# Dummy matmuls in the opening of an attention and SwiGLU kernel: one in fp32 for every four in bf16

## The chip, the cores and the metric

The kernel runs on one core of one Trainium2 chip. The metric is the device time of one execution in microseconds (us). Several executions are timed; the median is quoted. A ratio is the mean time of one kernel's fast runs over that of the other's fast runs in the same rounds, so it is not quite the ratio of the medians quoted beside it. Brackets after a ratio hold its 95% interval. One early execution of the kernel before took 565.97 us; it is no fast run and enters no ratio, though the medians of 3 and 4 runs below count it.

## The reference

Causal attention over a sliding window of 64 keys, for 8 batches of 8 heads with 576 tokens and head size 64. Then a SwiGLU block with 512 model and 1536 hidden columns.

```python
scores = q @ k.transpose(0, 1, 3, 2) / sqrt(D)
mask = (rel >= 0) & (rel < 64)               # rel = query position - key position
attn = softmax(where(mask, scores, -1e9))
x = (attn @ v).transpose(0, 2, 1, 3).reshape(B * S, H * D)
g = x @ w_gate
out = (g * sigmoid(g) * (x @ w_val)) @ w_out
```

## The kernel before

The matmuls run in bf16. Inputs arrive in fp32, are cast on VectorE (DVE), ScalarE (ACT) or GpSimd (POOL), and queries and keys of the opening are transposed on TensorE (PE). While the first loads are still coming, PE is given dummy matmuls on zeros, so that its clock is released and stays released.

```python
wz = cst.tile([P, 512], BF16, name="wz")
...
def warm(n):
    w_ps = ps_f.tile([P, 512], FP32, name="w_ps", tag="g")
    for _ in range(n):
        nc.tensor.matmul(w_ps[:], wz[:, 0:P], wz[:])

def begin():
    dve.memset(wz[:], 0.0)
    make_identity(nc, identb[:])
    dve.memset(masks[0][:], 1.0)
    ...
# the opening (cut to the dummies and what stands beside them)
cast_k(0, "k_f", pool)
warm(11)
turn2(0, "k_f", (act, dve))      # transposes of the first keys
...
warm(3)
turn2(0, "q_f", (act, dve))
warm(3)
scores(0, True)
...
warm(7)
turn2(1, "k_f", act)
...
warm(4)
products(1)
...                              # then warm(1), warm(2), warm(2)
```

`keys_last` is a VectorE copy of keys that a transposing DMA has just been asked for:

```python
finish()
if n + 4 < NG // 2:
    turn1(n + 4, "k_f")          # DMA transposes
    keys_before(n + 4)
    keys_last(n + 4)             # copy on VectorE
project(t - 1, s)
```

The softmax here doesn't subtract the row's maximum and nothing guards it: scores larger than these inputs give would overflow.

## Time and profile before

| | before |
|---|---|
| median | 338.15 us (337.53 at best), 3 runs |
| span of the profiled run | 336.3 us |
| PE busy | 97% of the span |
| PE idle in the first 35 us | 5.65 us |
| PE idle from 36 us to its last matmul (333.2 us) | 0.76 us, one wait |

PE sets the time. Apart from 3.0 us after its last matmul, its idle time is almost all in the first 35 us, where it waits for casts and those for loads. The prediction shows the lines. The table of waits between 254 and 268 us names its parts (columns: who waited for whom, us in total, times, longest):

```profile
DVE kL L145 <- DMA kT<-k_fb: 3.4, 1, 3.4
PE g_ps L316 <- DVE sg L327: 0.8, 1, 0.8
```

VectorE stands in `keys_last` for 3.4 us until a transposing DMA lands; behind it in VectorE's order stands the gate multiplication (sg) that would free PE's next PSUM buffer.

### The profile page before, as it was taken

Reading aid. Unit: us, or ns where it says so; the run is one execution under the profiler, and the core shown is the slowest. Engines: PE = TensorE matmul, PEld = TensorE weight load, DVE = VectorE, ACT = ScalarE, POOL = GpSimd, SP = SyncE. Lnnn points to the kernel's source line nnn. Section 1 sums busy time; section 2 is a strip of 40 time slices with the busy share of each in tenths; the row PEclk is TensorE's granted clock in tenths of the full one; section 3 lists DMA queues with packets and bytes.
Section 4 is the critical chain, followed back from the end, with each engine's and each line's share of the span. In section 5 each row is a group of like instructions: output and inputs, shape, how many; then the busy total and the mean of one; then the engine's idle time right before and its main releaser. Section 6 shows DMA issues by size and latency. Waiting matters only on the chain.

```text
span 336.3 us, 7201 instructions
## 1 busy us (share of the span) xinstructions
PE 326.8 (97%) x2731; PEld 163.3 (49%) x2731; DVE 227.5 (68%) x491; ACT 152.0 (45%) x268; POOL 100.8 (30%) x148
## 2 busy tenths in 40 slices
PE   7898999999999999999999999999999999999996
PEld 3555665545544444444444444444444444444444
DVE  4667898995676767677868677767665866655520
ACT  3858876566525252534343434343433434232222
POOL 4543455661053333333333333223333110000000
DMA  8999999979968988899889698979998420211013
GB/s 207 266 308 283 309 274 320 317 168 230 206 137 166 181 165 172 165 188 167 178 174 168 152 180 175 164 141 214 146 188 137 101 64 32 65 31 31 33 47 109
DMA packets 150610, 56.83 MB, mean 169 GB/s; under 512 B 124720, under 2 KB 144560, under 8 KB 150576
## 3 DMA queue, kind: packets, MB, share of 16 engines
q1 hardware_dynamic: 150576, 56.38, 77.5%
q8 instruction: 21, 0.34, 0.5%
q14 instruction: 13, 0.11, 0.2%
HBM read 37.75 MB, written 9.44 MB: 140 GB/s over the span
## 4 chain that ended last, share of the span: by engine, by line
PE 85%; DMA 7%; ACT 2%; DVE 2%; SPq 1%; issue 1%; DVEq 0%; ACTq 0%
PE g_ps L316 26%; PE o_ps L334 26%; PE v_ps L316 25%; DMA q_f<-in_q_dram 3%; PE ao_ps L252 3%; PE s_ps L221 2%; DMA v_f<-in_v_dram 2%; PE tp L170 1%; DMA kT<-k_fb 1%; ACT E L234 1%; SPq L89 1%; DMA out_dram<-os__4900 1%; DVE sg L327 1%; PE xtp L276 1%; ACT ve L118 0%
## 5 line engine op out<-in xcount | busy, mean ns | idle before, releaser
L316 PE MATMUL g_ps<-xT,wg 128*128 128x512 bf16 (+1 forms) x460 | 112.4, 367 | 1.3 <-DVE sg L327 1.3
L316 PE MATMUL v_ps<-xT,wv 128*128 128x512 bf16 (+1 forms) x460 | 112.1, 366 | 0.5 <-POOL wv L120 0.3
L327 DVE SCALAR_TENSOR_TENSOR sg<-th,g_ps 128x512 f32<-128x512 f32 (+1 forms) x115 | 75.0, 652 | 52.1 <-ACT th L321 51.9
L321 ACT ACTIVATE th<-g_ps 128x512 f32<-128x512 f32 (+1 forms) x115 | 65.8, 573 | 77.6 <-PE g_ps L316 74.9
L334 PE MATMUL o_ps<-wo,hT 128*128 128x512 bf16 (+2 forms) x456 | 98.5, 368 | 0.0
L328 DVE TENSOR_TENSOR hT<-sg,v_ps 128x512 bf16<-128x512 f32 (+1 forms) x115 | 75.4, 655 | 11.9 <-PE xtp L276 0.5
L316 PEld LDWEIGHTS <-wv 128*128 128x128 bf16 x460 | 44.6, 98 | 49.6 <-ACT wv L118 0.7
L334 PEld LDWEIGHTS <-hT 128*128 128x128 bf16 x456 | 43.6, 98 | 49.5
L316 PEld LDWEIGHTS <-wg 128*128 128x128 bf16 x460 | 41.8, 98 | 43.4 <-issue 1.7
L234 ACT ACTIVATE E<-s_ps 128x512 bf16<-128x512 f32 x72 | 38.6, 596 | 8.1 <-PE s_ps L221 8.0
L120 POOL CAST q_fb<-q_f 128x1024 bf16<-128x1024 f32 x13 | 13.7, 1050 | 63.4 <-DMA q_f<-in_q_dram 37.9
L120 POOL CAST k_fb<-k_f 128x1024 bf16<-128x1024 f32 (+1 forms) x16 | 16.0, 1003 | 55.5 <-DMA k_f<-in_k_dram 44.2
L263 DVE TENSOR_TENSOR x_b<-ao_ps,r 128x256 bf16<-128x256 f32 x72 | 30.6, 425 | 2.5
L236 DVE TENSOR_TENSOR E<-E,mask 128x512 bf16<-128x512 bf16 x58 | 25.8, 472 | 9.0 <-ACT E L234 8.3
L120 POOL CAST ve<-v_f 64x512 bf16<-64x512 f32 x47 | 29.3, 623 | 2.9
L120 POOL CAST vo<-v_f 128x512 bf16<-128x512 f32 x30 | 19.0, 634 | 30.0 <-DMA v_f<-in_v_dram 29.8
L262 DVE RECIPROCAL r<-ao_ps 128x4 f32<-128x4 f32 x72 | 12.5, 174 | 4.6 <-PE ao_ps L252 4.6
L252 PEld LDWEIGHTS <-E 128*64 128x64 bf16 x576 | 11.0, 110 | 7.6 <-issue 5.8
L120 POOL CAST vL<-v_f 64x512 bf16<-64x512 f32 x15 | 9.3, 621 | 11.3 <-DMA v_f<-in_v_dram 10.5
L221 PEld LDWEIGHTS <-kT 64*128 64x128 bf16 x512 | 9.1, 95 | 5.7 <-issue 3.0
L252 PE MATMUL ao_ps<-vo,E 128*64 128x65 bf16 x256 | 11.9, 196 | 0.0
L252 PE MATMUL ao_ps<-ve,E 128*64 128x65 bf16 x256 | 11.9, 196 | 0.0
(100 smaller groups left out, 143.9 us busy)
## 6 DMA issues: line engine op xcount, KB each, us to landing
v_f<-in_v_dram SPq DMA_DIRECT2D x32, 256.0 KB, 4.5
k_f<-in_k_dram SPq DMA_DIRECT2D x20, 256.0 KB, 4.1
q_f<-in_q_dram SPq DMA_DIRECT2D x18, 256.0 KB, 5.1
q_f<-in_q_dram SPq DMA_DIRECT2D x7, 512.0 KB, 7.1
k_f<-in_k_dram SPq DMA_DIRECT2D x6, 512.0 KB, 7.4
w_f<-in_moe_w_gate_dram SPq DMA_DIRECT2D x6, 512.0 KB, 6.8
w_f<-in_moe_w_val_dram SPq DMA_DIRECT2D x6, 512.0 KB, 6.8
wo_f<-in_moe_w_out_dram SPq DMA_DIRECT2D x6, 512.0 KB, 7.2
```

The source lines that it names most:

```text
L120: eng.tensor_copy(y, x)
L221: nc.tensor.matmul(ps[a][:, p, b], keys, qT[g // 2 % QR][y, p, o:o + 64], tile_position=(64 * a, 0), start=not masked, stop=not masked or ...
L234: act.activation(e, x[:], AF.Exp, scale=0.125)
L236: dve.tensor_mul(e, e, mk[:].unsqueeze(1).to_broadcast([P, 4, 2, 64]))
L252: nc.tensor.matmul(o_ps[64 * b:64 * b + 64, i, :], Es[g % ER][:, y, b], z[:, y, :], tile_position=(0, 64 * b),)
L262: dve.reciprocal(r[:], o_ps[:, :, D])
L263: dve.tensor_mul(xb[g][:, 256 * h:256 * h + 256].rearrange("r (y d) -> r y d", y=4), o_ps[:, :, 0:D], r[:].unsqueeze(2).to_broadcast([P, 4 ...
L316: nc.tensor.matmul(ps[:, 0:n], w[:, c, P * m:P * m + P], xT[t][:, c, c0:c0 + n], start=(c == 0), stop=(c == 3),)
L321: act.activation(th[:, 0:n], g_ps[:, 0:n], AF.Tanh, scale=0.5)
L327: dve.scalar_tensor_tensor(sg[:, 0:n], th[:, 0:n], 1.0, g_ps[:, 0:n], ALU.add, ALU.mult)
L328: dve.tensor_mul(hT[t][:, m, c0:c0 + n], sg[:, 0:n], v_ps[:, 0:n])
L334: nc.tensor.matmul(o_ps[:, a:b], hT[t][:, c, P * s:P * s + P], wo[:, c, a:b], start=(c == 0), stop=(c == 11),)
```

## The change

Intent: an fp32 matmul of 512 columns keeps the array as long as four in bf16, with fewer instructions. PE's blocks of instructions then last longer while loads crowd the DMA engines.

```diff
     wz = cst.tile([P, 512], BF16, name="wz")
+    wz4 = cst.tile([P, 512], FP32, name="wz4")
...
     def warm(n):
         w_ps = ps_f.tile([P, 512], FP32, name="w_ps", tag="g")
-        for _ in range(n):
-            nc.tensor.matmul(w_ps[:], wz[:, 0:P], wz[:])
+
+        for z in [wz4] * (n // 4) + [wz] * (n % 4):
+            nc.tensor.matmul(w_ps[:], z[:, 0:P], z[:])
 
     def begin():
 
         dve.memset(wz[:], 0.0)
+        dve.memset(wz4[:], 0.0)
```

## The prediction

> **What bounds the kernel now.** I read the page first, then PE's instructions in order of time, then those of the other engines at the same moments. From the page (busy time by engine, the span in 40 slices, the DMA queues, the chain that ended last):
>
> ```profile
> PE 326.8 (97%) x2731; PEld 163.3 (49%) x2731; DVE 227.5 (68%) x491; ACT 152.0 (45%) x268; POOL 100.8 (30%) x148
> PE   7898999999999999999999999999999999999996
> DMA  8999999979968988899889698979998420211013
> q8 instruction: 21, 0.34, 0.5%
> PE 85%; DMA 7%; ACT 2%; DVE 2%; SPq 1%; issue 1%; DVEq 0%; ACTq 0%
> ```
>
> PE is the bound: it works from about 35 us to the end without a pause. Only the first four slices (8.4 us each) leave it idle time, and only there do the dummies run. So the change can act on the end only by moving the moment at which PE becomes saturated. PE in order of time, with the idle time before a group in brackets, says what holds it until then (columns: start, length, engine, line, what, count):
>
> ```profile
> 1.26 3.83 PE L347 MATMUL w_ps<-wz 128*128 128x512 bf16 x11 [1.26 <-DVE wz L351]
> 6.20 0.62 PE L170 MATMUL tp<-identb,k_fb 128*128 128x128 bf16 x8 [1.10 <-POOL k_fb L120]
> 9.43 1.68 PE L347 MATMUL w_ps<-wz 128*128 128x512 bf16 x7
> ...
> 12.74 0.62 PE L170 MATMUL tp<-identb,q_fb 128*128 128x128 bf16 x8 [0.95 <-DVE q_fb L120]
> ...
> 13.67 1.04 PE L347 MATMUL w_ps<-wz 128*128 128x512 bf16 x4
> ...
> 20.71 0.61 PE L316 MATMUL v_ps<-xT,wv 128*128 128x256 bf16 x4 [0.28 <-POOL wv L120]
> ...
> 23.81 1.02 PE L316 MATMUL g_ps<-xT,wg 128*128 128x512 bf16 x4 [0.51 <-DVE sg L327]
> ...
> 27.21 0.62 PE L170 MATMUL tp<-identb,q_fb 128*128 128x128 bf16 x8 [1.07 <-ACT q_fb L118]
> ```
>
> With two small ones not shown (0.16 before L208 at 16.25, 0.17 before L316 at 33.44) these pauses sum to 1.26+1.10+0.95+0.16+0.28+0.51+1.07+0.17 = 5.50 us. The table of seven windows of 5 us gives PE 29.34 us busy out of the first 35, so 5.66 idle: all but 0.16 us has a named data producer. I checked each producer's end against PE's start:
>
> ```profile
> 5.10 1.04 POOL L120 CAST k_fb<-k_f 128x1024 bf16<-128x1024 f32 x1 [0.91 <-DMA k_f<-in_k_dram]
> 19.61 1.04 POOL L120 CAST wv<-w_f 128x1024 bf16<-128x1024 f32 x1 [1.51 <-DMA w_f<-in_moe_w_val_dram]
> 26.54 0.62 ACT L118 CAST q_fb<-q_f 128x512 bf16<-128x512 f32 x1 [1.07 <-DMA q_f<-in_q_dram]
> ```
>
> 5.10+1.04 = 6.14 against 6.20; 19.61+1.04 = 20.65 against 20.71; 26.54+0.62 = 27.16 against 27.21. Each handover takes 0.05 to 0.06 us, and each cast waited for a load. The opening is bound by **loads**, and no pause is left that a late block of instructions could own.
>
> **What the Trainium skill says.** (1) "Runtime: NRT & Kernel Launch", section "Instruction fetch mechanics": instructions come in 16 KiB blocks of 256 through a DMA queue of the sequencer's own, the next block while the current one runs, mostly hidden. The trace agrees: 0.34 MB in 21 packets is 16 KiB each, PE's 2731+2731 = 5462 instructions are 21.3 such blocks, and no PE pause is unexplained. (2) "TensorE: Matmul & The Clock Gate", Part 1: the array runs at half clock until about 3.4 us of activity released it. The trace agrees: the first weight loads of the dummies start 0.43 us apart, and the last four lie within 0.80:
>
> ```profile
> 2.09 0.15 PEld L347 LDWEIGHTS <-wz 128*128 128x128 bf16 x1 [0.28 <-issue]
> 2.52 0.15 PEld L347 LDWEIGHTS <-wz 128*128 128x128 bf16 x1 [0.28 <-issue]
> 3.80 0.80 PEld L347 LDWEIGHTS <-wz 128*128 128x128 bf16 x4 [0.28 <-issue]
> ```
>
> The pitch of a 512-column matmul is thus 0.43 us cold and, from the L316 groups late in the chain (0.86 us for four), 0.216 warm; the clock is released near 4.1 us. (3) "FP8 and Floating Point Precision", section "TensorE Precision Notes": true FP32 takes four passes. The trace before has no fp32 matmul, so it cannot confirm it. (4) The clock-gate page, "Weight-path perf modes": the fast weight load is off for FP32. Not in this trace either; a bf16 load takes 98 ns.
>
> **The change part by part.**
>
> *Dummies.* The eight calls ask for 11, 3, 3, 7, 4, 1, 2 and 2: 33 bf16 matmuls. Now they give 2, 0, 0, 1, 1, 0, 0, 0 in fp32 and 3, 3, 3, 3, 0, 1, 2, 2 in bf16: 4+17 = 21. At four passes, one fp32 takes 4 x 0.216 = 0.86 us warm and 4 x 0.43 = 1.7 cold: the same array time. If its weight loads can't be hidden, I add one load per pass as a worst case, 4 x 0.098 = 0.39 us, so 1.26 us (estimates from the rows named).
>
> *Instructions.* In the compiled listing PE's rows go from 5464 to 5436: 12 fewer matmuls, 16 fewer weight loads, since an fp32 matmul has no load of its own there. That is 11% of one block of 256. What the chip makes of an fp32 matmul (one pair or several) I leave open. Between 15 and 20 us PE takes 93+88 instructions in 5 us, 36 per us, so the block boundary there moves 28/36 = 0.8 us later. As no pause belongs to a boundary, this is worth 0.
>
> *The new memset.* It is DVE's second instruction, ahead of the first fp32 dummy. The memset of 256 words took 0.27 us and that of 64 took 0.11, 0.83 ns a word, so 512 words cost about 0.27+256x0.00083 = 0.48, call it 0.5 us. PE starts at 1.76 instead of 1.26. Behind it, DVE's other memsets end near 3.7 instead of 3.2, long before DVE's first cast at 6.88. GpSimd's masks, built from two of them, ended at 4.19 and had 0.91 us to spare before k_f landed at 5.10; they end at about 4.7.
>
> *First group, 11 dummies' worth.* With release still at 4.1: (4.1-1.76)/0.427 = 5.5 units cold, 5.5 x 0.216 = 1.2 us warm, end at 5.3. Released 0.5 us later: 5.5. Both precede 6.20, where PE waited 1.10 us. If the clock stays cold throughout: 1.76+11x0.427 = 6.5, 0.3 late; the scores behind it end at 9.50 and their exponentials start only at 10.53, because ScalarE is still at a value cast that a load released. Absorbed.
>
> *The 7 at 9.43.* At worst 0.39 us longer. The transposes behind them end at 11.79; ScalarE copies them out from 12.46, and PE's next wait was 0.95 us. Absorbed.
>
> *The 4 at 13.67.* At worst 0.39 us longer, moving the products, normalisation and scores. PE had 0.28 us to spare at 20.71 and 1.07 at 27.21, where it waits for the q load that landed at 26.5. That load was issued at 15.49; what had to be free for it is from casts before 8 us, so no dummy delays it. Absorbed.
>
> Sum: 0 gained, 0 lost, some tenths either way where handovers shift. Predicted 338.1 us, the time before.
>
> **The rivals.**
>
> (a) *Fetches held PE in the opening, and longer blocks help.* For: DMA engines are 80 to 100% busy there, and instruction packets share them; one block came in during the first 20 us. Against: the accounting above leaves 0.16 us unowned, so at best about -0.2 us, and the 1.07 us wait at 27.21 would absorb even that. 338.0.
>
> (b) *fp32 dummies are slower than four bf16, through weight loads or more passes.* At 0.39 us each, 4 x 0.39 = 1.6 us of PE time, all absorbed as shown except for what crosses 27.21: 338.1 to 338.4. If they took double (0.86 us extra each), the last two could push about 0.9 us through 0.28+1.07 of slack; still below. Perhaps 338.5 with knock-on effects.
>
> (c) *The clock goes back to half, or is released late.* A later start, or fp32 work counted as less activity, could keep PE cold past 6 us; its scores, transposes and products up to 20 us would double. For: the start moves. Against: three bf16 dummies follow each fp32 group but one. Much of it hides under loads; I give it up to +1 us: 339.
>
> (d) *The saturation point is not set by loads alone*, because a shifted cast releases a buffer earlier or later. This shuffles tenths: +-0.4 us.
>
> **Range and chances.** Runs before were 337.53 and 338.15, and 338.0 profiled; the 565.97 is an outlier I do not compare with. Spread 0.3 us, plus (d) 0.4 and a tail to the slow side from (b) and (c): 337.3 to 339.0. Two per cent is 6.8 us, more than the 5.66 us that PE idles before 35 us, so faster by 2% is impossible by this path: 0.01. Slower by 2% needs five times my worst sum: 0.01. Within 2%: 0.98.
>
> **What would show it right or wrong.** Right: the first dummy starts near 1.8; an fp32 one takes about 0.86 us warm; the transposes of k_fb still start at 6.2 and those of q_fb at 27.2, still after their casts; idle in the first 35 us stays at 5 to 6 us; one block of instructions is fetched some 0.8 us later. Wrong: an idle stretch that vanishes without its producer ending earlier (fetch), the last dummy ending over 1 us late with the wait at 27.21 gone (slow fp32), or transposes after 6.2 at twice their pitch (cold clock).

## The result

| | before | after |
|---|---|---|
| median | 338.03 us, 4 runs | 337.89 us, 4 runs |
| span of the profiled run | 336.3 us | 336.2 us |
| ratio | | 1.0004 [0.9984, 1.0023] |

No difference beyond the interval. A second set, with five runs of the changed kernel, gave 337.68 against 337.81 us, ratio 0.9998 [0.9984, 1.0012]. The page of the changed kernel, in the lines that answer to those of the prediction:

```profile
PE 325.4 (97%) x2682; PEld 163.7 (49%) x2723; DVE 225.6 (67%) x492; ACT 152.3 (45%) x268; POOL 100.6 (30%) x148
q8 instruction: 21, 0.34, 0.4%
PE 84%; DMA 7%; DVE 3%; ACT 2%; issue 1%; SPq 1%; DVEq 0%; ACTq 0%
```

The weight loads (PEld) are fully recorded: 2731 before, 2723 now. Of the dummies' 33 loads 17 remained in bf16, so the four fp32 dummies made 2723 - (2731 - 33) - 17 = 8: two pairs of weight load and matmul each. The change saves 8 pairs, 16 instructions. (Some matmul records of this trace are missing, so I count loads.)

PE in order of time (start, length, instruction, count, idle time before it):

```profile
1.80 4.89 PE L349 MATMUL w_ps<-wz 128*128 128x512 f32 x7 [1.80 <-DVE wz L354]
6.53 0.61 PE L171 MATMUL tp<-identb,k_fb 128*128 128x128 bf16 x8
9.61 1.77 PE L349 MATMUL w_ps<-wz 128*128 128x512 f32 x4
...
12.80 0.62 PE L171 MATMUL tp<-identb,q_fb 128*128 128x128 bf16 x8 [0.95 <-DVE q_fb L121]
...
13.73 1.12 PE L349 MATMUL w_ps<-wz 128*128 128x512 f32 x2
...
23.59 1.02 PE L317 MATMUL g_ps<-xT,wg 128*128 128x512 bf16 x3 [0.53 <-DVE sg L328]
...
26.70 0.62 PE L171 MATMUL tp<-identb,q_fb 128*128 128x128 bf16 x8 [0.77 <-ACT q_fb L119]
```

The first dummies start 0.54 us later, and the transposes behind them 0.33 us later (6.53 against 6.20). By 12.80 that lateness is gone: 0.06 against 12.74. The query load near 27 us landed earlier this time, so PE enters its saturated part ahead. To follow that, I compared the start of each weight load with that of the same one in the trace before: PE is 0.52 us ahead at 28 us, 0.35 from 43 to 259 us, and 0.12 at the end. The lead shrinks at one place, PE's one wait after 36 us, which is 0.99 us long here in place of 0.76:

```profile
259.94 1.02 PE L317 MATMUL g_ps<-xT,wg 128*128 128x512 bf16 x3 [0.99 <-DVE sg L328]
```

Three questions follow. Is the lead of 0.35 us the change's? Is the long cold phase, until past 6 us, the fp32 form's? And what hides what the opening gains or loses?

### The profile page after: what moved, and what is told of

It reads as the page before. It is cut to its first block, busy times and chain, and to the rows that moved or that the text cites. A ratio compares the mean times of both kernels' runs of the same rounds, so it can differ in the third digit from the quotient of the medians.

```text
span 336.2 us, 7145 instructions
## 1 busy us (share of the span) xinstructions
PE 325.4 (97%) x2682; PEld 163.7 (49%) x2723; DVE 225.6 (67%) x492; ACT 152.3 (45%) x268; POOL 100.6 (30%) x148
## 4 chain that ended last, share of the span: by engine, by line
PE 84%; DMA 7%; DVE 3%; ACT 2%; issue 1%; SPq 1%; DVEq 0%; ACTq 0%
PE o_ps L335 26%; PE g_ps L317 26%; PE v_ps L317 25%; DMA q_f<-in_q_dram 3%; PE ao_ps L253 3%; PE s_ps L222 2%; DMA v_f<-in_v_dram 2%; PE tp L171 1%; DMA kT<-k_fb 1%; DVE sg L328 1%; ACT E L235 1%; DVE x_b L264 1%; SPq L90 1%; DVE hT L329 1%; DMA out_dram<-os__4890 1%
## 5 line engine op out<-in xcount | busy, mean ns | idle before, releaser
L317 PE MATMUL g_ps<-xT,wg 128*128 128x512 bf16 (+2 forms) x426 | 110.5, 366 | 3.3 <-DVE sg L328 1.5
L121 POOL CAST q_fb<-q_f 128x1024 bf16<-128x1024 f32 x13 | 13.7, 1050 | 63.4 <-DMA q_f<-in_q_dram 38.4
L237 DVE TENSOR_TENSOR E<-E,mask 128x512 bf16<-128x512 bf16 x58 | 24.4, 449 | 9.4 <-ACT E L235 8.7
L349 PE MATMUL w_ps<-wz 128*128 128x512 bf16 (+1 forms) x23 | 10.6, 577 | 1.9 <-DVE wz L354 1.8
```

What stands on the lines that cost most here:

```text
L121: eng.tensor_copy(y, x)
L237: dve.tensor_mul(e, e, mk[:].unsqueeze(1).to_broadcast([P, 4, 2, 64]))
L317: nc.tensor.matmul(ps[:, 0:n], w[:, c, P * m:P * m + P], xT[t][:, c, c0:c0 + n], start=(c == 0), stop=(c == 3),)
L349: nc.tensor.matmul(w_ps[:], z[:, 0:P], z[:])
```

## The experiments

### The two kernels again

No edit. What was expected of the changed kernel, then of the kernel before:

> The changed kernel once more, to see what varies from run to run. Theory (the opening is bound by loads, the change is absorbed): the time within 0.2% of the kernel before; the q_f transposes at 26.5 to 27.3 us, wherever the load lands; first transposes between 6.2 and 6.6. The release of the clock may fall elsewhere than in the first trace of this kernel (near 6.4 us)[...]. Rival (the change really brings the q load forward by 0.5 us): q_f transposes again near 26.7 us, and PE again 0.35 us ahead of the first trace of before from 45 to 259 us.

> The kernel before against itself: how far two runs of one program differ. Theory: ratio 1.000 within 0.002; q_f transposes anywhere from 26.5 to 27.3; the dummies' release of the clock anywhere between 3.4 and 7 us. Rival (the differences between the two first traces are the change's): q_f transposes again at 27.2 and the release again near 4.1 us.

Ratios to the kernel before: 0.9998 for the changed kernel, 1.0004 [0.9991, 1.0017] for the kernel before against itself. The second trace of the changed kernel:

```profile
6.32 0.61 PE L171 MATMUL tp<-identb,k_fb 128*128 128x128 bf16 x8
27.10 0.62 PE L171 MATMUL tp<-identb,q_fb 128*128 128x128 bf16 x8 [0.94 <-ACT q_fb L119]
```

The query load is back near 27.1, and this time PE is 0.30 us *behind* the first trace of before from 43 us to 259. So the lead of 0.35 us is no fixed effect of the change. The second trace of before had its query transposes at 26.95, not 27.21: the load itself wanders by some tenths.

### The late start alone, and the fp32 form alone

```diff
 late_bf16: the kernel before, bf16 dummies, begun as late as in the changed kernel
+    wz4 = cst.tile([P, 512], FP32, name="wz4")
+        dve.memset(wz4[:], 0.0)
         dve.memset(wz[:], 0.0)

 early_fp32: the changed kernel, fp32 dummies, begun as early as before
-    wz4 = cst.tile([P, 512], FP32, name="wz4")
+    wz4 = cst.tile([P, 256], FP32, name="wz4")
-        dve.memset(wz[:], 0.0)
         dve.memset(wz4[:], 0.0)
+        dve.memset(wz[:], 0.0)
     # moving operand of the fp32 dummies: the 256 columns twice, as [P, 2, 256]
```

> bf16 dummies as before, but begun after the extra 0.48 us memset, so at 1.8 us. Tells the late start from the fp32 form as the cause of the long cold phase (until about 6.4 us in the first trace of after). Theory ([...]any dummy counts): release at a time that differs from run to run, the 11 dummies end between 5.2 and 6.5 us, time within 0.2%. Rival 1 (fp32 counts as less activity): release near 4.1 to 4.6 us as before, dummies over by 5.6. Rival 2 (the late start misses a window): release again near 6.4.

> fp32 dummies begun as early as the bf16 ones before (memset of 256 fp32 words first, moving operand the same 256 columns twice, 512 columns in all), so from 1.26 us. Theory[...]: release somewhere between 3.4 and 7 us, fp32 halves 0.85 us cold and 0.43 warm, time within 0.2%. Rival (fp32 counts as less activity): release again after 6 us, the first transposes again at 6.5.

Both equal to before within their intervals: 337.95 us, ratio 1.0002 [0.9988, 1.0016], and 337.66 us, ratio 0.9996 [0.9982, 1.0010]. The weight loads of late_bf16 show its clock:

```profile
4.77 0.15 PEld L348 LDWEIGHTS <-wz 128*128 128x128 bf16 x1 [0.27 <-issue]
5.19 0.15 PEld L348 LDWEIGHTS <-wz 128*128 128x128 bf16 x1 [0.28 <-issue]
5.62 0.15 PEld L348 LDWEIGHTS <-wz 128*128 128x128 bf16 x1 [0.28 <-issue]
```

A pitch of 0.43 us is the cold one. Pure bf16 dummies from 1.80 us are thus still cold at 5.62, as the fp32 ones were. The kernel before, whose first trace released the clock near 4.1, was still cold at its weight load of 4.65 in its second trace. The run keys_later_before, which has the same opening, was cold at that of 5.08, and its first transposes still began cold: the eight take 0.78 us, between 0.62 in before (warm) and 1.03 in no_dummies (cold). So the release wanders over more than 2 us in one and the same opening, and no fp32 effect is needed to explain the changed kernel's long cold phase. With early_fp32 the first transposes began cold too, at 6.29, as its rival expected; but the bf16 dummies of keys_later_before did the same (keys_later_before, then early_fp32):

```profile
6.24 0.78 PE L170 MATMUL tp<-identb,k_fb 128*128 128x128 bf16 x8
6.29 0.71 PE L171 MATMUL tp<-identb,k_fb 128*128 128x128 bf16 x8
```

Whether fp32 dummies are counted exactly as bf16 ones these few traces can't tell. They do release the clock: in keys_later_after only fp32 dummies ran before the weight load at 5.29, the step to it from the load before is 0.77 us and not the cold 0.85 (see the next section), and the load behind it follows after 0.21:

```profile
4.52 0.15 PEld L349 LDWEIGHTS <-wz 128*128 128x128 bf16 x1 [0.52 <-issue]
5.29 0.32 PEld L349 LDWEIGHTS <-wz 128*128 128x128 bf16 x2 [0.61 <-issue]
```

### What one fp32 dummy costs

In the second trace of the changed kernel the fp32 dummy at 13.61 us is followed by the products at 14.66, 1.05 us. In the first trace of before, four bf16 dummies from 13.67 to 14.64 took 0.97. So warm it costs 0.08 us more than what it replaces. That surplus comes once per call: in plus_one (below) two in a row take 1.91 us, from 13.63 to 15.54, so the second takes 0.86. Cold, the weight loads of the changed kernel's first trace start as follows:

```profile
1.80 0.50 PEld L349 LDWEIGHTS w_ps<-wz 128*128 128x128 f32 x2 [1.80 <-DVE wz L354]
2.82 0.34 PEld L349 LDWEIGHTS w_ps<-wz 128*128 128x128 f32 x1 [0.52 <-issue]
3.67 0.34 PEld L349 LDWEIGHTS w_ps<-wz 128*128 128x128 f32 x1 [0.52 <-issue]
```

The starts from 2.82 on are 0.85 us apart, twice 0.43: each of the two halves of an fp32 dummy takes as long as two bf16 dummies.

### More dummies: how much slack is there

```diff
 plus_one, in the changed kernel          plus_three
-    warm(4)                              -    warm(4)
+    warm(8)                              +    warm(16)
     products(1)                               products(1)
```

> The changed kernel with one more fp32 dummy in the call at 13.7 us (8 in place of 4): 0.87 us more PE work there. Theory (the wait for the wv cast at 20.7, 0 to 0.5 us, and the wait for the q load near 27, 0.7 to 1.1, absorb it): the last wait shrinks to between 0 and 0.5, end +0 to +0.3 us. Rival (dummies are on the path that sets the end): +0.8 us or more.

> The changed kernel with three more fp32 dummies in the call at 13.7 us (16 in place of 4): 2.6 us more PE work there, more than the 0.7 to 1.6 us of slack behind it. Theory: both waits vanish, PE enters its saturated part 1.0 to 1.9 us later than before, and up to 0.8 us of that is given back at PE's one later wait, near 260 us: end +0.6 to +1.5 us. Rival (more slack than I counted, loads rule further on): under +0.4. Rival (each dummy counts in full): +2.4 or more.

plus_one: 338.28 us, ratio 1.0000 [0.9975, 1.0025]. PE in plus_one (first two lines) and in plus_three (the last):

```profile
23.91 1.02 PE L317 MATMUL g_ps<-xT,wg 128*128 128x512 bf16 x4 [0.17 <-DVE sg L328]
27.18 0.62 PE L171 MATMUL tp<-identb,q_fb 128*128 128x128 bf16 x8 [0.94 <-ACT q_fb L119]
```

```profile
26.02 1.02 PE L317 MATMUL g_ps<-xT,wg 128*128 128x512 bf16 x4 [0.53 <-DVE sg L328]
```

The extra 0.87 us is absorbed, but earlier than I expected: PE is 0.90 late at 15.7 us, 0.45 at 21.4 and on time at 27.7. It used up the wait at 20.7 and most of the one at 23.9, and left 0.94 of the wait near 27, which I had expected to shrink to 0.5 or less. plus_three: 339.13 us, ratio 1.0035 [1.0005, 1.0065]; 0.0035 of 338 is 1.2 us. Its 2.6 us of extra work become 2.66 us of lateness at 15.4, 2.20 at 21.2 and 1.17 at 27.4, where the wait has vanished. That is the slack behind 13.7 us, measured: 2.66 - 1.17 = 1.5 us.

### No dummies

```diff
-        for _ in range(n):
+        for _ in range(1 if n == 11 else 0):
             nc.tensor.matmul(w_ps[:], wz[:, 0:P], wz[:])
```

> All dummies gone but one. What the warm clock of the opening is worth at all, an upper bound for what a late release can cost. Theory (the opening is bound by loads): transposes, scores and products up to 15 to 20 us run at half clock, but most of that falls into pauses and into the time the dummies took; +0 to +1.5 us at the end. Rival (the clock rules the opening): +3 us or more.

337.93 us, ratio 0.9992 [0.9965, 1.0020]: no difference. The trace is that of the slowest of its four executions (338.86 us; the others took 337.13 to 338.06). It shows PE cold (eight transposes that took 0.62 us take 1.03) and 2.2 us behind just before 24 us. The waits that before has near 24 and 27 us take this back to 0.51 us by 28 us, where it stays until 55. Only then, at three waits for VectorE up to 66 us, does the lateness grow to 1.67 us, and at the wait near 260 it falls from 1.70 to 0.88. So most of what the cold opening cost was absorbed before 28 us. Whether the missing dummies cause the loss after 55 us is not shown.

### Taking the wait near 260 us away

```diff
             turn1(n + 4, "k_f")
             keys_before(n + 4)
-            keys_last(n + 4)
...  # one round of the loop later, behind that round's first finish()
+        if 8 < w and n + 3 < NG // 2:
+            keys_last(n + 3)
```

The copy goes on waiting for its DMA, but a round later, when the DMA has all but landed. It still stands ahead of the scores that read the keys.

> The changed kernel with VectorE's copy of the last keys (which waits 3 to 4 us for a transposing DMA and so holds up the gate multiplication, PE's one wait after 36 us) moved one round of the loop later. Theory (a lead or a delay from the opening is partly lost at that wait, 0.6 to 1.0 us long in all traces): the wait near 260 is gone, the lead PE has at 250 us reaches the end, 0.5 to 1.0 us faster than before (0.2 to 0.3%). Rival (the wait moves to the next thing that needs the keys, or the DMA is late for the scores): no gain.

> The same move in the kernel before, so that the two can be compared without the wait near 260. Theory: 0.5 to 1.0 us faster than before, and equal to the changed kernel with the same move within 0.2%. Rival (the wait hid a real difference between bf16 and fp32 dummies): the two differ by 0.3 us or more, in the direction of the lead that PE has at 45 us.

| | median | ratio to before |
|---|---|---|
| keys_later_after | 337.14 us | 0.9964 [0.9948, 0.9980] |
| keys_later_before | 337.17 us | 0.9965 [0.9949, 0.9981] |

Neither trace has a PE wait after 45 us. VectorE's wait in keys_last falls from 3.4 us to this:

```profile
DVE kL L145 <- DMA kT<-k_fb: 0.8, 1, 0.8
```

Both are faster than before, by 1.0 us in the medians and 1.2 by the ratio (0.0035 of 338), and equal to each other. The wait had not been hiding a difference between the two sorts of dummy. These two versions beat both kernels.

> No dummies but one, with the copy of the last keys moved as in the two runs before, so that the wait near 260 cannot take back what the opening loses. In the no_dummies trace PE was 1.7 us late at 70 us and 0.9 at the end. Theory (cold matmuls in the opening do cost about 1 to 1.7 us, hidden in the end time by the wait near 260): 0.8 to 1.8 us slower than keys_later_before (337.2), so about 338 to 339 us. Rival (dummies are worth nothing): equal to keys_later_before within 0.3 us, 337.2.

Without dummies and with the copy moved: 337.96 us, ratio 0.9995 [0.9978, 1.0012], against 0.9965 for the same move with dummies. In these two runs having dummies is worth about 0.3%, or 1.0 us, of which no_dummies showed nothing. They were run at other times. I compare their ratios to before, whose intervals just touch. How much of it is the clock is open. In this trace PE is 2.0 us behind just before 24 us, but only 0.33 at 28; the rest, up to 1.18, comes at a PE pause that the others lack, for a value cast on GpSimd:

```profile
44.11 0.19 PE L252 MATMUL ao_ps<-ve,E 128*64 128x65 bf16 x1 [0.79 <-POOL ve L120]
```

The value load behind it landed at 42.62, against 41.02 in before, and a block of PE's instructions was fetched from 39.52 to 40.54. Without the dummies PE also has 64 instructions fewer, so its blocks come at other times (next section). No run separates that from the clock.

### More instructions for the same array time

```diff
 quarters: four matmuls of 128 columns for each dummy
-        for _ in range(n):
-            nc.tensor.matmul(w_ps[:], wz[:, 0:P], wz[:])
+        for _ in range(4 * n):
+            nc.tensor.matmul(w_ps[:, 0:P], wz[:, 0:P], wz[:, 0:P])

 halves: two of 256 columns
+        for _ in range(2 * n):
+            nc.tensor.matmul(w_ps[:, 0:256], wz[:, 0:P], wz[:, 0:256])
```

> Each bf16 dummy of 512 columns becomes four of 128: the same array time, 132 pairs in place of 33, so 198 more instructions on PE, most of a block of 256. This moves block boundaries the other way than the change, and seven times as far or more. Theory (no pause in the opening belongs to a fetch): within 0.2% of before, pauses of the first 35 us still all after their casts, one or two more blocks fetched before 30 us. Rival (fetches held PE, which is what the change set out to help): new pauses without a producer, at least 0.5 us later at the end.

quarters: 338.32 us, ratio 0.9999 [0.9975, 1.0024]. The time did not move, but the opening did. GpSimd's cast of the second value tile, first in before and then in quarters:

```profile
12.99 0.61 POOL L120 CAST vo<-v_f 128x512 bf16<-128x512 f32 x1 [2.19 <-DMA v_f<-in_v_dram]
```

```profile
14.16 0.61 POOL L120 CAST vo<-v_f 128x512 bf16<-128x512 f32 x1 [3.40 <-DMA v_f<-in_v_dram]
```

In the thirteen other traces this cast starts between 12.89 and 13.05. In quarters the load is 1.2 us late, and the products on PE wait 0.80 us for the cast. What precedes it is a block of PE's instructions, fetched from 10.89 to 12.08: it took 1.19 us. I then sent halves to see whether that was chance:

> Each bf16 dummy becomes two of 256 columns: the same array time, 66 pairs in place of 33, 66 more instructions. In the run with quarters a block of instructions was fetched at 10.9 us for 1.2 us, and every load and issue behind it came 1.2 us later than in the ten other traces (first GpSimd cast of the second value tile at 14.16 in place of 12.9 to 13.05, gate weight issue at 12.64 in place of 11.3 to 11.5). Theory (a fetch among the loads delays the load stream by its own length, and not PE directly): the first fetch falls between 12 and 15 us, and the load whose packets are then in flight lands 1.0 to 1.4 us later than in before, those ahead of it on time; no PE pause without a producer; end within 0.3%. Rival (the delay in quarters was chance): cast at 12.9 to 13.1 and gate weights landing near 16.8 us as before, wherever the fetch falls.

halves: 339.86 us against 338.02, ratio 1.0059 [1.0036, 1.0082], slower by 1.8 us in the medians and 2.0 by the ratio. The SyncE queue that issues the loads, first in before and then in halves (start, length):

```profile
11.37 1.01 SPq L291 DMA_DIRECT2D w_f<-in_moe_w_gate_dram  x1
12.42 0.74 SPq L291 DMA_DIRECT2D w_f<-in_moe_w_val_dram  x1
```

```profile
11.41 2.44 SPq L291 DMA_DIRECT2D w_f<-in_moe_w_gate_dram  x1
13.89 0.80 SPq L291 DMA_DIRECT2D w_f<-in_moe_w_val_dram  x1
```

The issue that overlaps the fetch takes 1.4 us longer; the cast of the second value tile, whose load was ahead, starts on time at 13.01. These gate weights land at 17.84, against 16.75 in before. The records of PE's instruction queue in the traces give these times (us):

```
             pairs in dummies   first block fetched   second begins
before              33            15.90 to 16.98          23.94
after               25            15.69 to 16.76          23.98
after_again         25            15.93 to 17.01          23.93
halves              66            12.12 to 13.41          22.93
quarters           132            10.89 to 12.08          20.02
no_dummies           1            18.27 to 19.43          26.49
```

In before and no_dummies the same value-weight load is issued at 12.42 and 12.45. With the fetch at 15.90 it landed 7.1 us after issue; with the fetch at 18.27, 5.8 us (last column):

```profile
w_f<-in_moe_w_val_dram SPq DMA_DIRECT2D x1, 512.0 KB, 7.1
w_f<-in_moe_w_val_dram SPq DMA_DIRECT2D x1, 512.0 KB, 5.8
```

The ten traces with the first fetch between 15.69 and 16.15 all have 6.7 to 7.4 us here; none_keys_later, with it at 18.23, has 5.75. So the kernel before too has a load that is 1.3 us later where a fetch comes first. A later fetch does not speed up what follows, though: the next gate weights land at 21.04 in no_dummies and at 21.07 in before.

My expectation for halves was right on the loads around the first fetch and wrong on the end, which I had put within 0.3%. In its trace (of the slowest of its four executions) PE is 1.56 us behind at 27 us and 2.34 at 43: the next key load lands 1.95 us later than in before, the query load 1.56. (Of this trace's 3.3 us over before, 2.1 show at PE's last weight load; 1.1 more are a wait for an output store at the very end.) In quarters PE is 1.07 us behind from 43 to 259 us, and the wait near 260 takes 0.82 of it back; of halves' 2.68 it takes 0.54. So in these traces most of quarters' delay is given back, and most of halves' is not.

Why halves loses twice as much before 45 us I can't settle: every later block boundary moved as well in both. In halves the second fetch, 22.93 to 24.11, comes ahead of the late key load, which lands 3.2 us after the load before it; in no_dummies, with no fetch there, the two are 1.8 us apart. But late_bf16 has a fetch from 22.59 to 23.77, and there they are 1.7 us apart. So a fetch can hold up a load by about its own length, and need not. That fetches cause the 2 us of halves is argued from its one trace: no run moved a fetch and nothing else.

## Why the prediction was right

**Right on the time** (338.1 predicted, 337.89 measured) and on its core: the opening is bound by loads, the dummies lie in slack, and the end does not move. plus_one and plus_three give the slack behind the call at 13.7 us as 1.5 us, where the prediction counted 0.28 + 1.07 = 1.35.

**The memset** was sized exactly: 0.48 us, first dummy at 1.80 against 1.76 predicted. GpSimd's masks end at 4.73 (4.7 predicted).

**The cost of an fp32 dummy**: 0.08 us above four bf16 ones warm, against 0 in the base case and 0.39 at worst. That holds for one alone; one that follows another takes the 0.86 us of the base case.

**The first group** went the way of the fallback, not of the main case. The main case took the release at 4.1 us from one trace as if it belonged to the kernel. It wanders. (The prediction also found that trace in agreement with 3.4 us of activity; its own figures give 4.1 - 1.26 = 2.8.) What happened is the sentence "if the clock stays cold throughout: 6.5, 0.3 late": the transposes came at 6.53, 0.33 late, and were absorbed. Two of my marks of a right prediction were therefore wrong in the first trace: the transposes at 6.2, and idle in the first 35 us, 4.76 us rather than 5 to 6, as cold dummies count as busy. (The second trace has 6.32 and 5.19.) The query transposes, marked for 27.2, came at 26.70 and 27.10, after their casts.

**The step on instructions failed twice**, without harm to the time. The compiled listing has 28 rows fewer, the chip executes 16 instructions fewer, because each fp32 matmul becomes two pairs. And the block that should be fetched 0.8 us later was fetched at 15.69 and 15.93, against 15.90 before. Why even the 16 moved nothing is open.

**The reason given for that step was wrong.** I wrote that a block boundary is worth 0 because no pause of PE belongs to one, and bounded a gain at 0.2 us. PE indeed has no pause over 0.16 us without a producer in any trace. But a fetch can act on the loads: where the first fetch meets one, it lands 1.1 to 1.3 us later (quarters, halves, and before against no_dummies), and PE then waits for a cast, which looks like any wait for data. The accounting of pauses by producer can't see this. halves, with 66 instructions more, ended 2 us later, and its trace starts to fall behind, by 0.72 us at 17.5, after the first fetch has met the loads. So a boundary is not always worth 0. But this edit's 16 instructions did not move the first fetch, and that moving one later gains time is not shown.

**Rival (d)**, tenths from shifted handovers, is what the two traces of the changed kernel show: 0.35 us ahead in one, 0.30 behind in the other.

**What I overlooked** is the wait near 260 us. PE is not quite "without a pause" from 35 us on. That one wait can take back part of a gain or loss (0.23 of the 0.35 us of lead; 0.82 of no_dummies' 1.70 of lateness; only 0.08 of plus_three's). It is no rule: early_fp32, 0.32 us ahead in front of it, is 0.50 ahead behind it. Having the copy where it was cost about 1 us by itself.

## What to carry to other kernels

When a change in the opening leaves the time alone, look for the next wait downstream before concluding that the change does nothing: here a single copy behind a DMA held up PE at 260 us, and moving it gained about as much as having the dummies at all. Judge instruction counts in a load-bound stretch also by when blocks are fetched among the loads, not only by whether the engine ever waits for instructions. And take no event that wanders from run to run, such as the release of the clock, from a single trace.

## What the Trainium skill lacked or had wrong

- "Runtime: NRT & Kernel Launch", section "Instruction fetch mechanics", calls the cost of crossing a block mostly hidden. For PE itself every trace agrees (no pause over 0.16 us without a producer). It does not say that the 16 KiB packet takes 0.9 to 1.9 us among busy DMA engines (21 fetches in the trace of before), nor that a load can land about as much later when a block is fetched: the cast at 14.16 against 12.99 in quarters, though nothing of the kind at the second fetch of late_bf16.
- "FP8 and Floating Point Precision", section "TensorE Precision Notes", gives four passes for fp32. The time agrees (0.85 us cold for each half of 512 columns, 1.05 against 0.97 us warm). It does not say that the chip runs one fp32 matmul as two pairs of weight load and matmul, 8 loads for 4 matmuls here, while the compiled listing shows one row.
- "TensorE: Matmul & The Clock Gate", Part 1, puts the transition at around 4 us, ±500 ns from run to run, where it shows what one observes. The runs spread wider: release near 2.8 us after the first dummy in one trace of before, over 5 us (begun at 1.26, transposes still 0.11 us apart up to 6.54) in keys_later_before with the same opening. Its note further down, that the cold phase varies from run to run, fits.
